# Mask products of both query halves in four row groups, with parts of the v product between them

## The chip, the cores and the metric

The kernel runs on one core of one Trainium2 chip. The metric is the device time of one execution in microseconds. A core has a matrix engine (PE, which reads its operands from SBUF and writes to PSUM), a vector engine (DVE), a scalar engine (ACT), a third elementwise engine (POOL) and SyncE (SP). Each takes its instructions in the order in which the program puts them there; semaphores tie them together. DMAs are issued from the queues of SP, ACT and POOL.

## The reference

Two blocks in a row: an attention in which a query sees only the keys with the same 6-bit hash, then a two-layer feed-forward block with a learned slope.

```python
q_bits = (np.einsum('bhsd,dk->bhsk', q, proj) > 0)     # 4 batches, 8 heads, 768 tokens, width 64, 6 bits
k_bits = (np.einsum('bhsd,dk->bhsk', k, proj) > 0)
mask = q_bucket[:, :, :, None] == k_bucket[:, :, None, :]
scores = np.where(mask, scale * np.matmul(q, k.transpose(0, 1, 3, 2)), -1000000000.0)
attn = np.exp(scores - max); attn = attn / (sum(attn) + 1e-09)
x = np.matmul(attn, v)                                  # to (3072, 512)
h = x @ w_in
out = (np.maximum(h, 0.0) + alpha * np.minimum(h, 0.0)) @ w_out
```

All inputs and outputs are float32.

## The kernel before

`fast_path` does the work; `general_path` runs only if the inputs are out of the range that `fast_path` takes. Heads are taken in 16 **pairs** (`pi`), the two heads `s` of a pair on partitions 0 to 63 and 64 to 127. The loop over pairs is the attention stage, which takes the first 305 us or so; then the feed-forward stage begins, with the two layers in blocks.

Everything wrapped in `do(...)` keeps its program order on its engine. What isn't, most DMAs for instance, is put among it by the framework.

**One pair on PE.** The 768 keys are six key tiles `kc` of 128 (`NC`), the 768 queries are two halves `g` of 384 (`NCH`, `CW`). A *cell* is one `(kc, g)`; `CELLS` lists the twelve, `(0,0), (0,1), (1,0)` and so on.

- `scores` (L778), for each cell: first the **bit product**, one bf16 matmul for each head, then the full-precision product `kT` by `qT`, one float32 matmul for each head, added to the same PSUM tile (L786; each head's operands stand on 64 rows of the array). The bit product adds a penalty where the hashes differ, so that the exponential there is nothing. The bits of keys (`kb`) and queries (`qb`) take 12 of the 64 rows of each head; the rest is zero. ACT then takes the exponential of both heads at once into `pts[kc]` (L789).
- `hash_bits` (L727): the hash products of the next pair's keys and queries (L734), their signs on ACT (`hr`, L740), and six DMAs from POOL and two from ACT that bring them to `qb` and `kb` (L747). `qb` has two buffers, `kb` one.
- `attend` (L811): the product with v, the **v cells**. Twelve cells of four float32 matmuls, each on 32 columns of the array (L819), accumulate in `av`, which has one buffer in PSUM.
- `totals` (L825): eight products with ones (L832) of the summed exponentials into `sm`.

PSUM: a score tile takes two banks (`two_banks`, three buffers, which `hs` and `sm` share), `av` takes two.

**One pair on DVE and POOL.** `divide(pi - 1)` (L836) turns the totals of the previous pair into reciprocals: DVE's transpose `st` (L846), `rc`, `rr` and `vs` (L851); then on POOL `weight_sums`, which forms one difference of the first layer's weights (L664) if one is due, and four small copies that spread `rr` over partitions (L855, L856); then on DVE whatever is passed as `between`, the transpose `dn` (L858) and the quotient `x` (L864), which is the last reader of `av`. `x` goes to DRAM from SP. `between` is `weight_begin`: the transpose of the next pair's keys `kT` (L713, `turn_blocks`), two steps of rounding a piece of the weights (`weight_clamp` L611, `weight_parts` L617), in four pairs a difference of x's (`sum_x`), and the first addition of exponentials (`add_first`, `accp`, L797). Then follow on DVE the end of that weight piece (`weight_sum`, L642 and L645), the other additions (`add_third` L805, `add_last` L801 and L802, `add_total` L808), the second piece of the pair, and the transpose of the queries of the pair after the next. `load_weight` fetches further pieces from POOL's queue.

In program order a pair is: twelve score cells, `divide` of the previous pair with `weight_begin` inside it, weight work and additions, `hash_bits`, twelve v cells, `totals`.

Of the kernel before, what the change touches and what calls it, by code (L numbers as in the profile page):

```python
# [8 lines left out]
F32 = mybir.dt.float32  # L9
# [3 lines left out]
AF = mybir.ActivationFunctionType  # L13
# [394 lines left out]
def fast_path(  # L408
# [12 lines left out]
    nc = tc.nc  # L421
    P = 128
    B, H, S, D = q.shape
    NB = proj.shape[1]
# [4 lines left out]
    NC = S // P  # L429
# [3 lines left out]
    NCH = NC // CH  # L433
# [162 lines left out]
    def weight_abs(i, engine=None):  # L596
        i = order[i]
        lo, hi = halves(i)
        wx[i] = pool.tile([P, 512], F32, name=f"wx{i}", tag="wx")
        wr[i] = pool.tile([P, 512], I32, name=f"wr{i}", tag="wr")  # L600
        do(ACT.activation(wr[i], lo, AF.Copy, scale=2.0 ** -29))  # L601
        if engine is DVE:
            do(DVE.tensor_scalar(wx[i].bitcast(U32), hi, 0x7FFFFFFF, None, op0=ALU.bitwise_and))
            return
        do(ACT.activation(wx[i], hi.bitcast(F32), AF.Abs))
# [86 lines left out]
    def two_banks(name):  # L692
        return psum.tile([P, 2, 512], F32, name=name, tag="sc", bufs=3)
# [33 lines left out]
    def hash_bits(pi):  # L727

        both = two_banks(f"hs{pi}")
        ps = both[:, 0, :CW]  # L730
        for half in range(2):
            for n, name in enumerate("kq"):
                c = D * n + 32 * half
                do(PE.matmul(  # L734
                    ps[c : c + 32], wh2, tr[name, pi][:, half * CW : (half + 1) * CW], start=True, stop=True,
                ))
        if pi == 2:
            do(PE.transpose(both[:, 1, :NF], alpha16, ident[:NF, :NF]))
        raw = pool.tile([P, CW], BF16, name=f"hr{pi}", tag="hr", bufs=1)
        do(ACT.activation(raw, ps, AF.Sign, bias=hb2))  # L740
        if pi == 2:
            do(DVE.tensor_copy(alpha, both[:, 1, :NF]))
        bits["q", pi], bits["k", pi] = qbs[pi % 2], kb
        for name, half, queue in (("k", 0, nc.scalar), ("q", 0, nc.gpsimd), ("q", 1, nc.gpsimd), ("k", 1, nc.gpsimd)):
            for s in range(2):
                c = D * "kq".index(name) + 32 * half + NB * s
                queue.dma_start(  # L747
                    bits[name, pi][D * s : D * s + 2 * NB, half * CW : (half + 1) * CW], raw[c : c + 2 * NB],
                )

    def hash_first(half):

# [25 lines left out]
    def scores(pi, cells):  # L778
        for kc, g in cells:
            sc = two_banks(f"sc{pi}_{kc}_{g}")  # L780
            ks = slice(kc * P, (kc + 1) * P)
            qs = slice(g * CW, (g + 1) * CW)
            for what, first in ((bits, True), (tr, False)):
                for s in range(2):
                    r = slice(D * s, D * s + D)
                    do(PE.matmul(  # L786
                        sc[:, s, :CW], what["k", pi][r, ks], what["q", pi][r, qs], start=first, stop=not first,
                    ))
            do(ACT.activation(pts[kc][:, g, :, :CW], sc[:, :, :CW], AF.Exp, scale=SCALE / DOWN))  # L789


    def p(kc):
        return pts[kc].rearrange("p g s w -> p (g s) w")[:, :, :CW]

    def add_first(pi):
        accp[pi] = pool.tile([P, 2 * NCH, CW], F32, name=f"accp{pi}", tag="accp", bufs=1)
        do(DVE.tensor_tensor(accp[pi], p(0), p(1), op=ALU.add))  # L797
# [10 lines left out]
        do(DVE.tensor_tensor(accd[pi], accd[pi], accp[pi], op=ALU.add))  # L808


    def attend(pi):  # L811

        av[pi] = psum_av.tile([P, 2, 512], F32, name=f"av{pi}", tag="av")
        for kc in range(NC):
            for g in range(NCH):
                w = CW + 1 if g == 0 else CW
                for s in range(2):
                    for t in range(0, D, 32):
                        do(PE.matmul(  # L819
                            av[pi][D * s + t : D * s + t + 32, g, :w], nat["v", pi][:, s, kc * D + t : kc * D + t + 32],  # L820
                            pts[kc][:, g, s, :w], start=(kc == 0), stop=(kc == NC - 1),
                        ))
# [13 lines left out]
    def divide(pi, between=lambda: None):  # L836

        b, hp = pairs[pi]  # L840
        n = CW // 32
        a = pool.tile([P, CW], F32, name=f"st{pi}", tag="st", bufs=1)
        r = pool.tile([P, n], F32, name=f"rc{pi}", tag="rc")
        rr = pool.tile([P, NCH, n], F32, name=f"rr{pi}", tag="rr")
        d = pool.tile([P, NCH, CW], F32, name=f"dn{pi}", tag="dn", bufs=1)
        do(DVE.transpose(a, sums[pi][:, 0, :CW]))  # L846
        do(DVE.tensor_scalar(r, a.rearrange("p (n w) -> p n w", w=32)[:, :, 0], S * EPS, None, op0=ALU.add))
        for g in range(NCH):
            do(DVE.reciprocal(rr[:, g], r))
        vsum[pi] = pool.tile([P, 1], F32, name=f"vs{pi}", tag="vs")  # L850
        do(DVE.tensor_scalar(vsum[pi], av[pi][:, 0, CW : CW + 1], EPS, None, op0=ALU.mult))  # L851
        weight_sums(1, vsum[pi])
        for q0 in (0, D):
            q1 = q0 + 32
            do(POOL.tensor_copy(rr[q0 : q0 + 32, 1], rr[q1 : q1 + 32, 1]))  # L855
            do(POOL.tensor_copy(rr[q1 : q1 + 32, 0], rr[q0 : q0 + 32, 0]))  # L856
        between()
        do(DVE.transpose(  # L858
            d.rearrange("p g w -> p (g w)"),
            rr.rearrange("p g n -> p (g n)").unsqueeze(2).to_broadcast([P, NCH * n, 32]),  # L860
        ))

        x = mid.tile([P, NCH, CW], F32, name=f"x{pi}", tag="x", bufs=1)
        do(DVE.scalar_tensor_tensor(x, av[pi][:, :, :CW], vsum[pi], d, op0=ALU.add, op1=ALU.mult))  # L864
        nc.sync.dma_start(x_s[b, hp], x.rearrange("p g w -> p (g w)"))
# [641 lines left out]
    for pi in range(NPAIR):  # L1507
        i = 2 * pi
        if pi == 12:
            now_stored.append(pi)  # L1510

        def weight_end(i):
            weight_sums(1, weight_sum(i))
            weight_group(i)
            load_weight(i + 3)

        def weight_begin():
            if pi == 1:
                weight_end(1)
                turn_blocks(2, "q")  # L1520
            if pi + 1 < NPAIR:
                turn_blocks(pi + 1, "k")
            weight_clamp(i)
            weight_parts(i)
            if pi in (6, 9, 12, 15):
                sum_x(0, (6, 9, 12, 15).index(pi), DVE)
            add_first(pi)

        if pi:
            scores(pi, CELLS)  # L1530
            divide(pi - 1, weight_begin)
            if pi == 1:
                weight_abs(3)
        else:
            rest = [c for c in CELLS if c not in ahead]
            scores(pi, rest[:4])
            weight_abs(0, DVE)
            scores(pi, rest[4:])
            add_first(pi)
            weight_clamp(0)  # L1540
            weight_parts(0)
        weight_sum(i)
        weight_group(i)
        load_weight(i + 3)
        if pi > 1:
            weight_clamp(i + 1)
        add_third(pi)
        add_last(pi)
        add_total(pi)
        if pi == 0:  # L1550
            weight_abs(1, DVE)
            weight_clamp(1)
        if pi == 1:
            weight_clamp(i + 1)
        weight_parts(i + 1)
        if pi:
            weight_end(i + 1)
        if pi + 1 < NPAIR:
            hash_bits(pi + 1)
            do(ACT.activation(tr["q", pi + 1], tr["q", pi + 1], AF.Copy, scale=DOWN))  # L1560
        if 0 < pi < NPAIR - 2:
            turn_blocks(pi + 2, "q")
        attend(pi)
        if pi + 1 == NPAIR:
            now = ff1(0, 0)
            now.step(1)
        totals(pi)
        if pi + 1 == NPAIR:
            now.step(5)
            divide(pi)  # L1570
        else:
            weight_abs(i + 2)
        if pi + 2 < NPAIR:
            load(pi + 2, "v")
        while stores_due and pi < 10:
            stores_due.pop(0)()
        if pi in (9, 12, 15):
            load_w((9, 12, 15).index(pi))
        if pi in (3, 4, 6, 9):
            load_x(0, {3: 0, 4: 3, 6: 2, 9: 1}[pi])  # L1580
        for name in "qk":
            magnitude(pi, name)
            if pi + 3 < NPAIR:
                load(pi + 3, name)
        if stores_due and pi == 11:
            stores_due.pop()()
        if 0 < pi < NPAIR - 1:
            weight_abs(i + 3)
# [142 lines left out]
```

## Time and profile before

| | |
|---|---|
| median of 3 runs | 858.42 us (857.66 to 858.5) |
| the profiled execution | 859.28 us, its span 857.5 us |
| PE busy | 847.5 us, 99% of the span |
| DVE busy | 772.4 us, 90% |
| ACT busy | 405.5 us, 47% |
| POOL busy | 163.9 us, 19% |
| granted PE clock | 0.998 |
| score products in float32 (L786) | 768 matmuls, mean 482 ns |
| bit products (L786) | 384 matmuls, mean 324 ns |
| v products (L819) | 1536 matmuls, mean 485 ns |

The span is the time from the first to the last instruction of the profiled execution, which stands beside the time that the same execution took on the device. Matmuls are pipelined: one starts before the one before it has ended, and those on different rows or columns of the array overlap. So a duration in the table is not what a matmul adds; the distance from start to start is. The page's chain of waits is empty for this execution, so it is read from the engines' timelines.

### The profile page before, as it was taken

To read this page: it belongs to the slowest core of one execution; us is meant where nothing else is said; L and a number is where in the kernel's file an instruction comes from. 1 tells how busy PE (TensorE), PEld (TensorE's weight loads), DVE (VectorE), ACT (ScalarE), POOL (GpSimd) and SP (SyncE) were. 2 spreads that over 40 slices of the span, in tenths; PEclk is the share of its full clock that TensorE was granted. 3 is DMA by queue.
4 is the path that set the end of the run, shared out by engine and by line. 5 is a ranking of instruction groups with operands and counts; after the bars stand their busy time and mean duration, and the time that the engine had idled before them with its cause. 6 is when DMAs were issued, how large, how long until landed. Compare 5 with 4: busy or idle time off the path is not lost.

```text
span 857.5 us, 15370 instructions
## 1 busy us (share of the span) xinstructions
PE 847.5 (99%) x5674; PEld 600.0 (70%) x5674; DVE 772.4 (90%) x1251; ACT 405.5 (47%) x754; POOL 163.9 (19%) x321
## 2 busy tenths in 40 slices
PE   9999999999999999999999999999999999999996
PEld 4444444444445445559998769999778999687996
DVE  6999999999999987889998989998879998879996
ACT  7787788876867842331115441114452114352111
POOL 1322434424424401210006200002100000300001
PEclk9999999999999999999999999999999999999999
DMA  8965779879698437784444844335833435830242
GB/s 198 179 151 132 188 180 240 166 200 252 147 220 198 153 123 271 235 273 166 166 126 120 296 141 135 113 115 179 287 130 114 145 117 171 262 118 22 99 164 63
DMA packets 181765, 144.85 MB, mean 169 GB/s; under 512 B 121536, under 2 KB 161648, under 8 KB 178096
## 3 DMA queue, kind: packets, MB, share of 16 engines
q1 hardware_dynamic: 166496, 113.15, 46.7%
q0 software_dynamic: 12176, 29.29, 11.2%
q10 hardware_dynamic: 3008, 1.33, 0.6%
q8 instruction: 47, 0.77, 0.4%
q14 instruction: 38, 0.31, 0.1%
HBM read 111.16 MB, written 31.46 MB: 166 GB/s over the span
## 4 chain that ended last, share of the span: by engine, by line


## 5 line engine op out<-in xcount | busy, mean ns | idle before, releaser
L786 PE MATMUL sc<-qT,kT 64*128 64x384 f32 x768 | 155.1, 482 | 0.0
L789 ACT ACTIVATE pt<-sc 128x768 f32<-128x768 f32 x192 | 151.6, 810 | 3.4 <-PE sc L786 3.3
L819 PE MATMUL av<-pt,vn 128*32 128x385 f32 (+1 forms) x1536 | 127.1, 485 | 0.0
L819 PEld LDWEIGHTS av<-pt,vn 128*32 128x32 f32 x1536 | 50.2, 109 | 73.4 <-issue 70.0
L786 PEld LDWEIGHTS sc<-qT,kT 64*128 64x128 f32 x768 | 68.4, 187 | 35.8 <-issue 35.0
L1411 POOL DMA_DIRECT2D out_dram<-o x52 | 28.3, 553 | 337.9 <-DVE o L1404 336.4
L786 PE MATMUL sc<-qb,kb 64*128 64x384 bf16 x384 | 63.3, 324 | 0.6 <-DVE st L846 0.4
L976 DVE TENSOR_TENSOR g<-g,g 128x768 f32<-128x768 f32 (+1 forms) x80 | 62.8, 793 | 0.7
L1357 DVE TENSOR_TENSOR gs<-g,gs 128x768 f32<-128x768 f32 x56 | 53.3, 952 | 1.0
L1357 DVE TENSOR_TENSOR gs<-g 128x768 f32<-128x768 f32 x56 | 53.3, 951 | 0.0
L786 PEld LDWEIGHTS <-kb 64*128 64x128 bf16 x384 | 20.7, 94 | 36.2 <-issue 13.2
L1349 DVE TENSOR_TENSOR ws<-wl 128x512 f32<-128x512 f32 x56 | 38.4, 686 | 6.8 <-DMA wl<-w_out_s 6.8
L601 ACT ACTIVATE wr<-raw 128x512 int32<-128x512 uint32 x32 | 22.1, 691 | 32.7 <-DVE wso L645 17.0
L747 POOL DMA_DIRECT2D qb<-hr x60 | 30.1, 508 | 23.0 <-ACT hr L740 23.0
L797 DVE TENSOR_TENSOR accp<-pt,pt 128x1536 f32<-128x1536 f32 x16 | 28.1, 1758 | 4.3 <-ACT pt L789 4.3
L802 DVE TENSOR_TENSOR accd<-accd,pt 128x1536 f32<-128x1536 f32 x16 | 28.1, 1759 | 1.7
L808 DVE TENSOR_TENSOR accd<-accd,accp 128x1536 f32<-128x1536 f32 x16 | 28.1, 1758 | 0.6
L995 DVE SCALAR_TENSOR_TENSOR g<-h,alpha 128x384 f32<-128x384 f32 x39 | 23.9, 613 | 5.2 <-ACT h L988 4.9
L805 DVE TENSOR_TENSOR accp<-accp,pt 128x1536 f32<-128x1536 f32 x16 | 28.0, 1753 | 0.0
L801 DVE TENSOR_TENSOR accd<-pt,pt 128x1536 f32<-128x1536 f32 x16 | 28.0, 1751 | 0.0
L1560 ACT ACTIVATE qT<-qT 128x768 f32<-128x768 f32 x15 | 12.7, 844 | 26.4 <-DMA kb<-hr 17.4
L642 DVE SCALAR_TENSOR_TENSOR wx<-raw,wx 128x512 uint32<-128x512 uint32 x32 | 22.7, 709 | 0.5
(494 smaller groups left out, 1914.2 us busy)
## 6 DMA issues: line engine op xcount, KB each, us to landing
wi<-w_in_s SPq DMA_DIRECT2D x32, 512.0 KB
wl<-w_out_s SPq DMA_DIRECT2D x16, 1024.0 KB
wl<-w_out_r SPq DMA_DIRECT2D x12, 1024.0 KB
raw<-in_moe_w_in_dram POOLq DMA_DIRECT2D x15, 512.0 KB, 5.1
raw<-in_moe_w_out_dram POOLq DMA_DIRECT2D x14, 512.0 KB, 5.3
w_in_s<-wsi SPq DMA_DIRECT2D x16, 448.0 KB
qn<-in_q_dram SPq DMA_DIRECT2D x64, 96.0 KB
vn<-in_v_dram SPq DMA_DIRECT2D x16, 384.0 KB
```

The lines of the kernel that those rows point to most:

```text
L747: queue.dma_start(bits[name, pi][D * s : D * s + 2 * NB, half * CW : (half + 1) * CW], raw[c : c + 2 * NB],)
L786: do(PE.matmul(sc[:, s, :CW], what["k", pi][r, ks], what["q", pi][r, qs], start=first, stop=not first,))
L789: do(ACT.activation(pts[kc][:, g, :, :CW], sc[:, :, :CW], AF.Exp, scale=SCALE / DOWN))
L797: do(DVE.tensor_tensor(accp[pi], p(0), p(1), op=ALU.add))
L801: do(DVE.tensor_tensor(accd[pi], p(3), p(4), op=ALU.add))
L802: do(DVE.tensor_tensor(accd[pi], accd[pi], p(5), op=ALU.add))
L808: do(DVE.tensor_tensor(accd[pi], accd[pi], accp[pi], op=ALU.add))
L819: do(PE.matmul(av[pi][D * s + t : D * s + t + 32, g, :w], nat["v", pi][:, s, kc * D + t : kc * D + t + 32], pts[kc][:, g, s, :w], start=(k ...
L976: do(DVE.tensor_tensor(new_g(b, to)[:, at], g_m[b, x][:, at], g_m[b, y][:, at], op=ALU.subtract))
L1349: do(DVE.tensor_tensor(t, w2[b, n, x], w2[b, n, y], op=op))
L1357: do(DVE.tensor_tensor(t, g2[b, n, x], g2[b, n, y], op=ALU.subtract))
L1411: pinned(b + 1 < B and queue is nc.sync, queue.dma_start(out_v[b, ch * CH + c].rearrange("(w r) d -> r w d", r=32)[:, :, cols], src[32 * a ...
```

## The change

From the third pair on (`pi > 1`), the bit products of the last three key tiles are made for both query halves together. `hash_bits` puts a second copy of the key bits (columns of the last three key tiles) and of the query bits (second half) on rows 32 to 43 of each head's 64. The new `scores_both` multiplies 32 rows at a time: for each half and head one group of 32 rows, four matmuls into two PSUM tiles. Then come the float32 products and the exponential of each half as before. Before each of these three steps stands one v cell of the same pair, so `attend` runs in parts, and `CELLS[3:]` are left for its old place. `divide` of the previous pair now stands after the first six score cells in the program, with only `turn_blocks` as its `between`; the rest of `weight_begin` follows it. Pairs 0 and 1 keep their order; rows 32 to 63 of the key bits' first half are set to zero once.

```diff
@@ hash_bits
+        for name in "kq":
+            for s in range(2):
+                c = D * "kq".index(name) + 32 + NB * s
+                to = D * s + 32
+                nc.gpsimd.dma_start(bits[name, pi][to : to + 2 * NB, CW:], raw[c : c + 2 * NB])
@@
+    def scores_both(pi, kc):
+
+        sc = [two_banks(f"sc{pi}_{kc}_{g}") for g in range(NCH)]
+        ks = slice(kc * P, (kc + 1) * P)
+        for g in range(NCH):
+            for s in range(2):
+                r = slice(D * s + 32 * g, D * s + 32 * g + 32)
+                do(PE.matmul(
+                    sc[g][:, s, :CW], bits["k", pi][r, ks], bits["q", pi][r, g * CW : (g + 1) * CW],
+                    start=True, stop=False,
+                ))
+        for g in range(NCH):
+            for s in range(2):
+                r = slice(D * s, D * s + D)
+                do(PE.matmul(
+                    sc[g][:, s, :CW], tr["k", pi][r, ks], tr["q", pi][r, g * CW : (g + 1) * CW],
+                    start=False, stop=True,
+                ))
+            do(ACT.activation(pts[kc][:, g, :, :CW], sc[g][:, :, :CW], AF.Exp, scale=SCALE / DOWN))
@@
-    def attend(pi):
+    def attend(pi, parts):
 
-        av[pi] = psum_av.tile([P, 2, 512], F32, name=f"av{pi}", tag="av")
-        for kc in range(NC):
-            for g in range(NCH):
+        if pi not in av:
+            av[pi] = psum_av.tile([P, 2, 512], F32, name=f"av{pi}", tag="av")
+        for kc, g in parts:
+            if True:
@@ weight_begin
             if pi == 1:
                 weight_end(1)
                 turn_blocks(2, "q")
-            if pi + 1 < NPAIR:
                 turn_blocks(pi + 1, "k")
@@ the loop over pairs
-        if pi:
+        if pi > 1:
+            scores(pi, CELLS[:6])
+            divide(pi - 1, lambda: turn_blocks(pi + 1, "k") if pi + 1 < NPAIR else None)
+            weight_begin()
+            for kc in range(3, NC):
+                attend(pi, CELLS[kc - 3 : kc - 2])
+                scores_both(pi, kc)
+        elif pi:
             scores(pi, CELLS)
             divide(pi - 1, weight_begin)
-            if pi == 1:
-                weight_abs(3)
+            weight_abs(3)
         else:
...
+            for s in range(2):
+                do(POOL.memset(kb[D * s + 32 : D * s + 64, :CW], 0.0))
...
-        attend(pi)
+        attend(pi, CELLS[3:] if pi > 1 else CELLS)
```

## The prediction

> **What bounds the kernel now.** I read the page's busy shares and slices first, then the timelines of PE, DVE and POOL through one pair of heads, then the DMA answers for the mask bits. The page says which engine is full:
>
> ```profile
> PE 847.5 (99%) x5674; PEld 600.0 (70%) x5674; DVE 772.4 (90%) x1251; ACT 405.5 (47%) x754; POOL 163.9 (19%) x321
> PE   9999999999999999999999999999999999999996
> PEclk9999999999999999999999999999999999999999
> ```
>
> PE has no gap and the full clock, so whatever PE issues more, or waits for, in the attention stage is added to the time. Matmul rows overlap, so I count from start to start. This is the PE timeline of one pair's end and the next one's start (columns: start us, us, engine, line, operation, names, shapes, count):
>
> ```profile
> 76.39 0.32 PE L786 MATMUL sc<-qb,kb 64*128 64x384 bf16 x2
> 76.55 0.81 PE L786 MATMUL sc<-qT,kT 64*128 64x384 f32 x4
> 77.29 0.51 PE L734 MATMUL hs<-kT,wh 128*32 128x384 f32 x1
> ...
> 77.64 0.49 PE L734 MATMUL hs<-kT,wh 128*32 128x384 f32 x1
> ...
> 77.96 7.94 PE L819 MATMUL av<-pt,vn 128*32 128x385 f32 x96
> 85.71 0.83 PE L832 MATMUL sm<-accd,ones 128*32 128x384 f32 x8
> 86.48 0.34 PE L786 MATMUL sc<-qb,kb 64*128 64x384 bf16 x2
> 86.65 0.81 PE L786 MATMUL sc<-qT,kT 64*128 64x384 f32 x4
> 87.29 0.33 PE L786 MATMUL sc<-qb,kb 64*128 64x384 bf16 x2
> ```
>
> Within one shape nothing is lost: bits to full precision 0.165 (86.48 to 86.65), full precision to the next bits 0.642, so 0.807 a cell; a v cell is 7.75/12 = 0.646. Where the shape changes, something is: 76.55 to 77.29 is 0.74 for 0.642 of work, and 85.71 to 86.48 is 0.77 for the 0.645 that eight such products take. A change of shape costs 0.10 to 0.125. A pair has two of them: 12 x 0.807 + 0.10 + 0.67 + 7.75 + 0.77 = 18.97, and the sm rows of successive pairs do lie 18.98 apart.
>
> DVE runs through the same pair with hardly more room (its timeline):
>
> ```profile
> 87.03 0.54 DVE L846 STREAM_TRANSPOSE st<-sm 128x384 f32<-128x384 f32 x1
> 88.09 0.10 DVE L851 TENSOR_SCALAR vs<-av 128x1 f32<-128x1 f32 x1
> 88.11 0.97 DVE L713 STREAM_TRANSPOSE kT<-kn 128x768 f32<-128x768 f32 x1
> 89.00 0.65 DVE L611 TENSOR_SCALAR_CACHE_REDUCE wx<-wx 128x512 f32<-128x512 f32 x1
> ...
> 92.45 0.97 DVE L858 STREAM_TRANSPOSE dn<-rr 128x768 f32<-128x768 f32 x1
> 93.45 1.02 DVE L864 SCALAR_TENSOR_TENSOR x<-av,vs,dn 128x768 f32<-128x768 f32 x1
> ```
>
> Between vs and dn stands POOL, which spreads the reciprocals and, in 8 of the 14 pairs that change, first forms a weight sum (its timeline):
>
> ```profile
> 88.46 1.28 POOL L664 TENSOR_TENSOR wsi<-wsi 128x512 f32<-128x512 f32 x1
> 89.81 0.36 POOL L855 COPY rr<-rr 32x12 f32<-32x12 f32 x1
> 90.20 0.19 POOL L856 COPY rr<-rr 32x12 f32<-32x12 f32 x1
> 90.44 0.19 POOL L855 COPY rr<-rr 32x12 f32<-32x12 f32 x1
> 90.67 0.19 POOL L856 COPY rr<-rr 32x12 f32<-32x12 f32 x1
> ```
>
> POOL ends at 90.86, 2.67 after vs. DVE doesn't notice: kT, the clamp, the shift and the 1.76 accp addition lie between. PE doesn't notice either: x ends at 94.47, and the next v product, which overwrites av, starts at 96.94.
>
> **The change part by part**, for a pair from 2 to 15. T is the start of its first score (86.48 here).
>
> *Bits.* Three times, two steps of 0.165 become one: -3 x 0.165 = -0.495. That four row groups run side by side is shown by no row; two row groups do here, and four column groups do (four hs products start within 0.02). From below the gain is 0, from above 0.495; the rows nearest to it say full, which I take.
>
> *Changes of shape.* v cells (128*32) now stand between scores (64*128), with 32-row bits between. In order: scores, v, bits, scores, v, bits, scores, v, bits, scores, hash: 11 changes with the one at the start, against 2. Of the nine added, six are between shapes that the rows show, at 0.10 to 0.125. Three go from 32-row bits to 64-row scores, which nothing shows: from below 0, since both span 128 columns; from above the largest change in the trace, f_0a to sm, 1.49 from start to start for 1.29 of work, 0.20. I take 0.12, as every change of shape in the trace lies near it. Sum 9 x 0.12 = 1.08. With the bits +0.585 a pair, x 14 = +8.2.
>
> A rule of the Trainium skill speaks against the change here: "TensorEngine Tiling (Array Packing)", Key Properties, says that going to another tiling mode, not just another tile, drains the engine. The rows above agree with it for the shapes that they hold; by the rule all nine changes count, and without it the three that no row shows could be left out, which would make the sum 42 x 0.12 = 5.0 less. "TensorE: Matmul & The Clock Gate", Measured speedup vs the span model, has four row tiles at 3.07 times, not 4; a step would then be an estimated 0.165 x 4/3.07 = 0.215, and the sum 42 x 0.05 = 2.1 more.
>
> *divide() ahead of the weight work, v before the last keys.* The first v cell overwrites av, so PE must now wait for x before the seventh score cell. PE comes there at T + 6 x 0.807 + 0.11 = T + 4.95. x: the totals end 0.06 after T (85.71 + 0.83), st starts 0.05 later (hs to its reader takes as much), vs ends 1.16 on, POOL 2.67, dn at once (0.03), x ends 2.02 after: T + 5.99, and some 0.06 to PE. PE stands 1.1 in the eight pairs with a sum. In the six without, POOL needs 0.93 (126.24 to 127.12), x is there at T + 4.3, and nothing waits. Queued behind the waiting product are all bits and scores of three key tiles and the hash; ACT's exponentials of these and DVE's accd wait for them in turn.
>
> The other side of it: DVE lost its cover and stands from kT's end (89.00) to 90.89, 1.9 a pair. Its own work is 18.3 (18.98 less 0.66 of waiting), so its round is 20.2 with a sum. PE's is 18.98 + 0.585 + 1.1 = 20.7: DVE keeps up, comes to st on time, and it is PE that waits. Its last work of a pair ends some 0.4 before the next totals are there. The addition of accd with the last key tile starts at T + 14.2, just when its last exponential ends.
>
> *POOL and the bits.* Four more DMAs a pair, 0.51 each, behind the six on POOL. They end 2.0 later, 0.4 before the next T; the weight load (0.55) and the sum of the pair's end (0.18, 1.28) come behind them, so that in six pairs vs finds POOL busy some 0.2 longer. Waits for x: 2 x 1.1 + 6 x 1.3 = +10.0.
>
> The last DMA starts 1.8 + 9 x 0.5 = 6.3 after the hash. In the quietest pairs one lands 1.6 after its issue; in the others the first takes 2 to 6.4 and the rest follow at 0.17 to 0.2. So the tenth lands 7.9 to 9.9 after the hash. The second score cell, which reads its rows, comes 0.67 + 9 x 0.646 + 0.77 + 0.81 = 8.06 after. Laid over the first landings of the 14 pairs this makes 5 in all, of which all but 1.1 falls where PE would wait for x anyway: +1.1. From below 0; from above 0.8 in each pair, 11.
>
> *At nothing:* the two memsets of kb (at most 0.74 each, the row of qb's, covered by POOL's wait for hr; 1.5 once without); turn_blocks of k, which stays at its place; the store of x on SP, which only moves forward; the v tile, loaded a pair ahead; psum, as scores_both needs two of three buffers and ACT, at 0.78 a cell, catches up during the v cells.
>
> **Sum:** 8.2 + 10.0 + 1.1 = 19.3. The profiled execution took 859.28, with a span of 857.5; the span becomes 876.8. The median of the runs is 858.42, 0.9 less than that execution: 877.7, said as 878.
>
> **Rivals.**
> - *Only the changes of shape.* x comes in time, as in the pairs without a sum, for instance if POOL's copies run before its sum. For: six pairs behave so. Against: the order on POOL stands in divide(). 858.4 + 8.2 + 1 = 868.
> - *The bits land late.* If each DMA takes the middle 4.0 from its own issue, the last lands 1.8 + 4.5 + 4.0 = 10.3 after the hash, 2.25 late in every pair, and the wait for x hides in it: 858.4 + 8.2 + 31.5 = 898. Against: the DMAs of one group now land 0.2 apart though issued 0.5 apart.
> - *Four row groups don't run together.* The change then doesn't do what it says: 877.7 + 6.9 = 885.
> - *Faster: the changes of shape are free at the new places.* If a change costs nothing when the next weights go to other rows, PE gains 14 x 0.495 = 6.9, hence 851.5. It decides below 0.495/9 = 0.055 a change, and only if x is early too: with x as late as above it ends at 861.5. Against: every change in the trace, whatever its rows and columns, costs 0.09 or more.
>
> **How the numbers follow.** Forecast 0.62, only shapes 0.16, late bits 0.12, four groups not together 0.04, free changes 0.06. The likeliest gives 878. Its low end: six changes at 0.105, three at 0, 8 waits of 0.9: 858.4 + 1.9 + 7.2 = 867.5. Its high end: nine at 0.14, waits of 1.5, landings 11: 858.4 + 10.7 + 12 + 11 = 892. I widen to 866 for the second case; what is left out is most of the late bits and the faster case, some 0.17. A difference under 0.2%, 1.7, can't be told from none. Of the free changes' 0.06, 0.01 is within that: faster 0.05, same 0.02, slower 0.93.
>
> **What would show it.** Right: the stretch from v cell to 32-row bits to scores has some 0.12 over its work at each step; PE's first v cell waits some 1.1 on DVE's x in eight pairs; dn waits on POOL some 1.9 there; sm rows lie 19.5 apart without a sum and 20.7 with one. Wrong: no gap at the changes, or bits of 0.33 for four, or a wait of the second score cell on a DMA in most pairs, or st waiting on nothing while sm waits on accd, which would make DVE the bound.

## The result, and the profile after

The changed kernel takes 971.8 us (median of 6 runs, 966.2 to 974.1) against 858.6: 1.131 times as long, interval 1.128 to 1.134. The forecast was 878, with a range up to 892. It is slower, as forecast, but by far more: 113 us lost where 19 were forecast.

The page of the changed kernel, its lines for PE, the granted clock, and the costliest wait of PE (line, engine, operation, names, shapes, count | busy us, mean ns | idle before, and what ended it):

```profile
PE 895.9 (92%) x5674; PEld 615.6 (63%) x5674; DVE 777.1 (80%) x1251; ACT 403.3 (41%) x754; POOL 184.7 (19%) x383
...
PE   9978778788887788999999999999999999999997
...
PEclk9978888998887889999999999999999999999999
...
L791 PE MATMUL sc<-qb,kb 64*128 64x384 bf16 x216 | 54.1, 394 | 68.0 <-DMA qb<-hr 67.9
```

PE, which had no gap before, now has gaps in the attention stage, and its clock is no longer full there. 68 us of the gaps end with a DMA from `hr` to `qb`: a copy of the query bits. The timeline of PE shows where it stands, from the end of one pair on:

```profile
241.98 0.83 PE L858 MATMUL sm<-accd,ones 128*32 128x384 f32 x8
242.74 0.34 PE L791 MATMUL sc<-qb,kb 64*128 64x384 bf16 x2
242.91 0.81 PE L791 MATMUL sc<-qT,kT 64*128 64x384 f32 x4
243.56 0.32 PE L791 MATMUL sc<-qb,kb 64*128 64x384 bf16 x1
247.65 0.47 PE L791 MATMUL sc<-qb,kb 64*128 64x384 bf16 x1 [3.77 <-DMA qb<-hr]
247.65 1.75 PE L791 MATMUL sc<-qT,kT 64*128 64x384 f32 x4
249.09 0.63 PE L791 MATMUL sc<-qb,kb 64*128 64x384 bf16 x2
249.41 1.59 PE L791 MATMUL sc<-qT,kT 64*128 64x384 f32 x4
250.69 0.63 PE L791 MATMUL sc<-qb,kb 64*128 64x384 bf16 x2
```

It is the second score cell, the first that reads the second half of the queries. Its first head goes ahead at 243.56; the other head stands for 3.8 until its copy has landed. And the cells after it come at 249.09 and 250.69, 1.60 apart, where 0.807 is the rule: PE runs at half its clock. Why the copy is late stands in POOL's timeline of the same pair (the DMA rows are their issue):

```profile
237.29 1.98 POOL L747 DMA_DIRECT2D qb<-hr  x4 [6.56 <-ACT hr L740]
239.26 1.24 POOL L747 DMA_DIRECT2D kb<-hr  x2
240.49 0.98 POOL L754 DMA_DIRECT2D kb<-hr  x2
241.47 0.51 POOL L754 DMA_DIRECT2D qb<-hr  x1
241.96 0.54 POOL L587 DMA_DIRECT2D raw<-in_moe_w_out_dram  x1
242.50 0.50 POOL L754 DMA_DIRECT2D qb<-hr  x1
```

The ten copies don't stand together. The weight load of 512 KB (L587) has been put in ahead of the last one; in pairs with a sum due POOL's sum goes in there as well. From issue to landing the trace has for the ninth copy (241.47), and then for the tenth (242.50), 9 KB like it but behind the load:

```profile
DMA to landing us min/median/max: 1.6/1.6/1.6
```

```profile
DMA to landing us min/median/max: 5.1/5.1/5.1
```

Thirteen of the 14 changed pairs have a load ahead of the last copy (in pair 2, of the last three), and their second cell waits 3.3 to 6.4. In the last pair no load is due: there the tenth copy lands 3.1 after its issue and the cell waits 1.2.

The granted clock in three stretches around that wait (stretch: length, busy of PE, PEld, DVE, ACT, POOL with instructions, PEclk, DMA share, GB/s):

```profile
238.00:245.70 7.70, 5.88 (x67) 2.19 (x60) 7.33 (x13) 5.65 (x10) 5.75 (x14) 1.00 0.40 102
245.70:252.50 6.80, 4.85 (x19) 3.09 (x20) 3.17 (x6) 1.62 (x2) 0.00 (x0) 0.50 1.14 334
252.50:259.00 6.50, 6.50 (x53) 2.78 (x50) 5.33 (x6) 4.19 (x6) 0.54 (x1) 1.00 0.91 166
```

Some 1.8 us into the wait (from 243.9) the clock is halved, and it stays so for 6.8, of which PE works nearly 5.

By the last totals the changed kernel is 115.7 behind (430.2 against 314.5). PE's gaps make 67 of it. The order of the products makes 11: where nothing waits a pair takes 19.84 in the second run below, against 18.98, 13 times (pair 2 took 19.90 before). Of the other 37 most is the clock: through the stage it is halved for 96 us, and PE works in some 63 of these, half of which, 32, is what it loses. Some 6 are not put down to anything.

### The profile page after: what moved, and what is told of

Its sections match the earlier page's. It is cut to its first block, busy times and chain, and to the rows that moved or that the text cites. A ratio compares the mean times of both kernels' runs of the same rounds, so it can differ in the third digit from the quotient of the medians.

```text
span 972.3 us, 15503 instructions
## 1 busy us (share of the span) xinstructions
PE 895.9 (92%) x5674; PEld 615.6 (63%) x5674; DVE 777.1 (80%) x1251; ACT 403.3 (41%) x754; POOL 184.7 (19%) x383
## 4 chain that ended last, share of the span: by engine, by line
## 5 line engine op out<-in xcount | busy, mean ns | idle before, releaser
L845 PE MATMUL av<-pt,vn 128*32 128x385 f32 (+1 forms) x1536 | 135.8, 488 | 0.0
L791 PE MATMUL sc<-qT,kT 64*128 64x384 f32 x432 | 120.1, 616 | 0.0
L791 PE MATMUL sc<-qb,kb 64*128 64x384 bf16 x216 | 54.1, 394 | 68.0 <-DMA qb<-hr 67.9
L845 PEld LDWEIGHTS av<-pt,vn 128*32 128x32 f32 x1536 | 45.8, 109 | 80.2 <-issue 79.8
L791 PEld LDWEIGHTS sc<-qT,kT 64*128 64x128 f32 x432 | 56.1, 244 | 50.0 <-issue 50.0
L810 PE MATMUL sc<-qT,kT 64*128 64x384 f32 x336 | 65.6, 509 | 0.0
L810 PEld LDWEIGHTS sc<-qT,kT 64*128 64x128 f32 x336 | 29.0, 186 | 18.0 <-issue 7.3
L884 DVE STREAM_TRANSPOSE dn<-rr 128x768 f32<-128x768 f32 x16 | 15.6, 978 | 18.5 <-POOL rr L882 18.0
```

The costliest lines, as they stand in the source:

```text
L791: do(PE.matmul(sc[:, s, :CW], what["k", pi][r, ks], what["q", pi][r, qs], start=first, stop=not first,))
L810: do(PE.matmul(sc[g][:, s, :CW], tr["k", pi][r, ks], tr["q", pi][r, g * CW : (g + 1) * CW], start=False, stop=True,))
L845: do(PE.matmul(av[pi][D * s + t : D * s + t + 32, g, :w], nat["v", pi][:, s, kc * D + t : kc * D + t + 32], pts[kc][:, g, s, :w], start=(k ...
```

## The experiments

Theory Q: the tenth copy lands late because the weight load stands ahead of it on POOL's queue, PE stands at the second cell, and the clock halves. Rival S: the changes of shape and the wait for x. Rival C: four more copies a pair are late wherever they stand.

**Which copy is last (e1).**

```diff
-        for name in "kq":
+        for name in "qk":
             for s in range(2):
                 c = D * "kq".index(name) + 32 + NB * s
```

> The changed kernel with the second copies of the query bits issued ahead of those of the key bits, so that the one copy that falls behind the weight load on POOL's queue is a key copy, which is not read before the seventh score cell. Theory Q (the query copy lands late because a 512 KB weight load and a POOL sum stand in front of it, PE stands at the second score cell, and the clock halves after that): the waits of the second cell go, the granted clock is 1.00 through the attention stage, and the time falls to 875 to 890. Rival S (the added changes of shape and the wait for x make the loss): it stays at 960 to 980. Rival C (four more copies a pair are late wherever they stand): it stays above 930.

Measured: 896.6, 1.044 times the time before (1.043 to 1.046). Two thirds of the loss go with the order of four small DMAs. It is over the 890 that Q named: four cells still wait for query copies (8.5 us), late key copies hold up a few bit products of 32 rows (1.5 us of PE, 2.7 of its weight loads), and the wait for x, up to 1.2, shows again. After the two longest of these waits (4.6 and 3.0) the clock is halved, for 10 us together. Q stands against S and C; C would have been above 930.

**Another queue for the copies (e2).**

```diff
-                nc.gpsimd.dma_start(bits[name, pi][to : to + 2 * NB, CW:], raw[c : c + 2 * NB])
+                nc.sync.dma_start(bits[name, pi][to : to + 2 * NB, CW:], raw[c : c + 2 * NB])
```

> The changed kernel with the four second copies issued from SP's queue in place of POOL's. Theory Q: no wait of the second score cell on a copy, clock 1.00, 873 to 885, a little under the run with the order swapped, as POOL is free for its sum and copies. Rival S: 960 to 980. Rival C: above 930, as the copies still share the DMA engines.

Measured: 885.5, 1.030 (1.027 to 1.032). Apart from three pairs with 1.8 to 4.1 of waiting and a halved clock after it, pairs take 19.84 without a sum of weights and 20.79 with one. In those three POOL issued its weight load ahead of at least the last of SP's copies; in the other eleven it issued it after all four, or none. So this run also has the two smaller terms pure: 0.86 a pair for the order of the products, 0.95 for the wait for x.

**v cells between, no row groups (e3).**

```diff
-        for name in "kq":
-            for s in range(2):
-                c = D * "kq".index(name) + 32 + NB * s
...
-                scores_both(pi, kc)
+                scores(pi, [(kc, 0), (kc, 1)])
```

> The changed kernel without the row groups: no second copies, the bits of the last three key tiles in 64 rows as before, one v cell ahead of each of these tiles, divide early. It adds six changes of shape a pair at 0.14 to 0.15 and the wait for x in the eight pairs where POOL has a sum due. Theory Q: 872 to 884, clock 1.00. Rival S: above 940.

Measured: 876.0, 1.020 (1.018 to 1.022), all by clock 1.00. Pairs take 19.71, and 20.66 with a sum. The wait for x is plain in its timeline of PE:

```profile
91.94 0.81 PE L786 MATMUL sc<-qT,kT 64*128 64x384 f32 x4
93.62 0.85 PE L840 MATMUL av<-pt,vn 128*32 128x385 f32 x8 [0.87 <-DVE x L885]
94.41 0.34 PE L786 MATMUL sc<-qb,kb 64*128 64x384 bf16 x2
```

The v cell would have come at 92.68, 0.74 after the score; it starts at 93.62.

**The copies alone (e4).** The kernel before, with the copies and the memsets and nothing else.

```diff
+        for name in "kq":
+            for s in range(2):
+                c = D * "kq".index(name) + 32 + NB * s
+                to = D * s + 32
+                nc.gpsimd.dma_start(bits[name, pi][to : to + 2 * NB, CW:], raw[c : c + 2 * NB])
...
+            for s in range(2):
+                do(POOL.memset(kb[D * s + 32 : D * s + 64, :CW], 0.0))
```

> The kernel before with nothing but the four second copies of the bits (and the memsets); the order of the pairs and the products stay. Theory Q: the last copy stands behind the weight load and POOL's sum here too, so the second score cell waits 4 to 7 in most pairs and the clock halves after it: 940 to 985. Rival S: 857 to 862. Rival C: 900 to 985, so this run tells Q and C from S, and the first two runs tell Q from C.

Measured: 952.4, 1.110 (1.108 to 1.113). Four DMAs of 9 KB a pair, which no product needs here, cost 94 us: 83% of the change's loss. (The products read the rows that the copies fill, so they wait.) In the last pair, where no load is due, the tenth copy lands 1.6 after its issue, nothing waits, and the pair takes 19.94 as before. The page of this run:

```profile
PEclk9988889898898898999999999999999999999999
...
L791 PE MATMUL sc<-qb,kb 64*128 64x384 bf16 x384 | 84.3, 358 | 61.9 <-DMA qb<-hr 61.9
```

**The weight load off the queue (e5).**

```diff
-    def load_weight(i, queue=nc.gpsimd):
+    def load_weight(i, queue=nc.sync):
```

> The changed kernel with the weight loads inside the loop issued from SP's queue, the ten bit copies staying on POOL's queue in the changed kernel's order. Theory Q (what holds the last copy is the 512 KB load ahead of it on the same queue): the last copy lands 1.6 to 3 after its issue, the second cell waits under 1 in most pairs, clock near 1.00, 873 to 890. Rival C2 (POOL's own queue of ten copies is too slow, load or not): above 930.

Measured: 910.5, 1.060 (1.057 to 1.062): over Q's 873 to 890, under C2's 930. In nine pairs the last copy lands 1.6 to 3.0 after its issue and the cell waits at most 1.2; in none of them did SP issue a weight load in the 6 us ahead of that copy. In the other five the cell still waits 2 to 6. In four of these SP had issued a load 0.8 to 4.8 ahead of the last copy, and the copy took 4.1 to 5.7, though the load now stood on another queue (in the fifth the load was 5.4 ahead, and the copy took 3.7). One of the four, in the timelines of SP, POOL and PE:

```profile
245.56 0.33 SPq L587 DMA_DIRECT2D raw<-in_moe_w_in_dram  x1
245.87 1.03 POOL L754 DMA_DIRECT2D qb<-hr  x2
250.14 0.70 PE L791 MATMUL sc<-qb,kb 64*128 64x384 bf16 x2 [2.06 <-DMA qb<-hr]
```

So a load issued ahead of the copy holds it up, and Q's words "on the same queue" are not borne out: what helped the nine pairs is that the load came after their copies. The load of the DMA engines plays a part too: they are busy for 0.86 to 0.99 of the stretch in three of the five pairs, where even the first copies take 5, and for about half in the other two, against 0.25 to 0.35 in pairs with short waits. That is read from the trace, and no run shows it by itself.

**Row groups alone (e6).** Bits of both halves in 32 rows, copies from SP, `divide` and all v cells at their old places.

```diff
-            divide(pi - 1, lambda: turn_blocks(pi + 1, "k") if pi + 1 < NPAIR else None)
-            weight_begin()
             for kc in range(3, NC):
-                attend(pi, CELLS[kc - 3 : kc - 2])
                 scores_both(pi, kc)
+            divide(pi - 1, lambda: (turn_blocks(pi + 1, "k") if pi + 1 < NPAIR else None, weight_begin()))
...
-        attend(pi, CELLS[3:] if pi > 1 else CELLS)
+        attend(pi, CELLS)
```

> Row groups alone: the last three key tiles by 32-row bits for both halves, no v cell between, divide and all v cells at their old places, second copies from SP. Shape theory from the runs so far: a tile loses about 0.10 from scores to 32-row bits and 0.21 from there to scores and gains 0.165, so +0.43 a pair, 864 to 866, and no wait for x. Rival (PSUM): with no v cell to cover them, two score tiles at once out of three buffers make PE wait for ACT, 0.3 a tile or more: 868 to 880, with waits of PE on ACT's exponentials in the trace.

Measured: 876.7, 1.021 (1.020 to 1.023), every changed pair 20.26 but the last (21.22, 19.94 before). The rival was right. Its PE timeline:

```profile
95.09 1.56 PE L810 MATMUL sc<-qT,kT 64*128 64x384 f32 x8
96.58 0.67 PE L803 MATMUL sc<-qb,kb 32*128 32x384 bf16 x4
97.18 1.56 PE L810 MATMUL sc<-qT,kT 64*128 64x384 f32 x8
```

The four bit products take 0.60 here against 0.27 with a v cell ahead: the second of the two score tiles is not free yet. ACT's timeline has its two exponentials on the tiles before from 96.05 to 97.56, the first until 96.86; two of the four bit products start at 96.58, the other two at 96.91. The v cells between are worth these 0.33 a key tile.

**POOL's sum after its copies (e7).** On e3:

```diff
-        weight_sums(1, vsum[pi])
         for q0 in (0, D):
...
             do(POOL.tensor_copy(rr[q1 : q1 + 32, 0], rr[q0 : q0 + 32, 0]))
+        weight_sums(1, vsum[pi])
```

> The third run (v between, bits in 64 rows) with POOL's weight sum put after the four small copies in divide. If the 0.95 by which the pairs with a sum are longer there is the wait for x behind POOL's sum, all pairs take 19.71: 858.6 + 14 x 0.73 = 869, 867 to 871, and PE's v cell waits on nothing. Rival (the wait is DVE's own lateness or the shapes): it stays at 874 to 877.

Measured: 869.0, 1.012 (1.010 to 1.014). Nearly all pairs take 19.71. The 0.95 was POOL's sum in the chain from `vs` to x, 7 us in all.

**Cells of the first half first (e8).**

```diff
-            scores(pi, CELLS[:6])
+            scores(pi, [(kc, g) for g in range(NCH) for kc in range(CH)])
```

> The changed kernel with the first six score cells in the order of the halves, so that three cells, not one, stand ahead of the one that reads the late copy; queue and copies as in the changed kernel. Theory Q: each wait is 1.6 shorter, about 3 to 4 a pair less than 5, and the clock loss shrinks more than in proportion, as waits below some 3.4 leave the clock alone: 905 to 945. Rival (the halved clock has another cause than the wait, such as 32-row products): the granted clock stays at 0.95 over the run, and only the 22 of shorter waits are gained, 947 to 953.

Measured: 943.1, 1.100 (1.096 to 1.105). PE's waits on the copies fell from 68 to 45, as expected from 1.6 a pair; the time the clock is halved fell from 96 to 61, not more than in proportion. Half the expectation failed: waits of 2.0 to 2.4 still halve the clock.

**Both waits taken away (e9).** The changed kernel with the edits of e1, e2 and e7 together.

> The changed kernel with both kinds of wait taken away: the second copies from SP with those of the queries first, and POOL's weight sum after the four small copies. What is left is the row groups, the nine changes of shape and the v cells between: 19.84 a pair against 18.98, so 858.4 + 14 x 0.86 = 870.5; with one or two pairs whose copies are still late behind other traffic 870 to 880. No wait of a v cell on x. If the row groups or the order gained anything that the waits had hidden, it would be below 866.

Measured: 872.5, 1.015 (1.014 to 1.017). Of the 14 changed pairs eleven take 19.84, one 20.15, the last 20.80 (19.94 before), and one 23.75, as SP issued its copies behind other loads. What is left is a loss by the shapes: the idea itself costs some 11 us (0.86 in 13 pairs).

**The wait filled (e10).** Twenty repeats of a bit product ahead of the second cell, whose result is overwritten.

```diff
+            for _ in range(20 if pi > 1 and (kc, g) == (0, 1) else 0):
+                for s in range(2):
+                    r = slice(D * s, D * s + D)
+                    do(PE.matmul(sc[:, s, :CW], bits["k", pi][r, ks], bits["q", pi][r, :CW], start=True, stop=True))
```

> The changed kernel with twenty repeats of a bit product (3.3 of PE work, its result overwritten) ahead of the second score cell of each changed pair, where PE otherwise stands waiting for the late copy. If the halved clock is caused by that standing and costs some 35 of the 113 by itself, the clock stays at 1.00 or nearly so and the time falls to 932 to 950 though PE does more; the waits that are left are about 1 to 3 a pair. Rival (the clock halves for another reason, or the slow cells hide in the wait): the time rises or stays, 965 to 1015.

Measured: 957.6, 1.116 (1.113 to 1.119). More work for PE, 14 us less time than the changed kernel. The expected range was missed: I took the waits for 3 to 6 and thought that 3.3 of filling would leave too little to halve the clock; in seven of 14 pairs it left 2 to 3, and the clock was still halved, for 27 us in place of 96. The DMAs are the same in this run, so their traffic isn't what halves the clock. That the clock follows PE's standing is shown; its price, some 32 to 36, is worked out and was not measured free of the waits.

No version of this idea beats the kernel before, so none was run as such.

## Why the prediction was wrong

*What bounds the kernel* was right: PE, with nothing to spare. So was the reading that each wait and each change of shape adds to the time.

*The step that failed* is the one on POOL and the bits. It put the four copies "behind the six on POOL", and then "the weight load (0.55) and the sum of the pair's end (0.18, 1.28) come behind them". It took the order in which the copies and the load stand in the timeline before for the order after. There the load came 3.8 after the last of six copies:

```profile
98.06 2.00 POOL L747 DMA_DIRECT2D qb<-hr  x4 [1.83 <-ACT hr L740]
100.06 1.00 POOL L747 DMA_DIRECT2D kb<-hr  x2
104.85 0.55 POOL L587 DMA_DIRECT2D raw<-in_moe_w_in_dram  x1 [3.79 <-DVE wx L642]
```

They are not wrapped in `do(...)`, so their place is not the program's, and the tenth copy went behind a 512 KB load. It was priced at +1.1, from above 11; the waits measured 67, and 62 with the copies alone. The prediction had named the sign of it, "a wait of the second score cell on a DMA in most pairs". The rival of late bits had the right place, the second cell, but took 4.0 from issue to landing, and 0.12 of the chance; it gave 898. Neither had a term for the clock, 32 to 36 more. With such a wait in every pair the forecast's bounds could not hold.

*Changes of shape*: right in kind, low in size: +11 for a forecast of +8.2. Nine changes and the bits came to 0.86 a pair where 0.585 was forecast. By its parts, in the PE timeline of e9 (a float32 product stands there as two matmuls, one after the other):

```profile
92.84 0.81 PE L791 MATMUL sc<-qT,kT 64*128 64x384 f32 x4
93.58 0.85 PE L845 MATMUL av<-pt,vn 128*32 128x385 f32 x8
94.36 0.34 PE L803 MATMUL sc<-qb,kb 32*128 32x384 bf16 x4
94.63 1.56 PE L810 MATMUL sc<-qT,kT 64*128 64x384 f32 x8
96.12 0.85 PE L845 MATMUL av<-pt,vn 128*32 128x384 f32 x8
```

Scores to v is 0.74 for 0.645: 0.10. v to bits is 0.78 to 0.79 for 0.646: 0.14; the prediction counted this among the changes that its rows show, but none of them holds 32-row bits. Bits to scores is 0.27: 0.105, if the step itself takes the 0.165 of two row groups. And the eight score products take 1.49 to the next v cell, for 1.29 and the 0.10 of that change, another 0.10: the first of their four steps takes 0.43, not 0.32. The second weight load starts 0.11 after the first there, where the later ones start along with the matmul before; that this is the reason is not shown. So from 32-row bits to float32 scores the price is 0.21, just over the bound of 0.20; I took 0.12. Three times 0.10 + 0.14 + 0.21 less 0.165 is the 0.86. The rule of the Trainium skill, "TensorEngine Tiling (Array Packing)", Key Properties, held at all nine places, those without a row among them.

*The bits* were right: four row groups do run together (their starts lie within 0.01, and each takes 0.33 as in the two groups before). But a step saved is 0.165 and a change of shape into scores costs 0.21: row groups lose 0.13 a pair even with the v cells between (19.84 against 19.71).

*The wait for x* was right in mechanism and near in size: 0.95 in eight pairs, 7 us, for 1.1 to 1.3 and 10. In the changed kernel itself it doesn't show: the second cell has waited longer already. DVE's wait on POOL, 1.64 in e3, is the 1.9 that was forecast for an early st.

*The faster rival*, free changes, is out: each change cost 0.10 to 0.21.

## What to carry to other kernels

A small DMA that another engine waits for must be placed by what is issued ahead of it, on its own queue or on another, and where a framework orders it, the order has to be read after the change, not taken from the trace before: here copies of 9 KB, the last of them issued behind 512 KB, cost 94 us by themselves. A wait of PE cost more than its length here once it filled half of a clock stretch. And here a step saved by row groups, 0.165, did not pay the two changes of shape around it, 0.14 and 0.21; whether a longer run of products in the new shape pays was not tried.

## What the runs showed of the hardware

The granted clock changed only at steps of a grid of 3.41 us, counted from the trace's clock marks. Taking the full-speed stretches of that grid in the attention stages of the changed kernel and its variants, every one with 1.79 us or more of PE standing was followed by half the clock (over 50 of them, in seven kernels), and none with 1.69 or less was (30 with over 0.7); two lie between, 1.73 and 1.76, one of each kind. So about half a stretch of standing is enough. In e8, for instance (stretches as above):

```profile
77.60:81.00 3.40, 1.77 (x14) 1.04 (x12) 2.95 (x5) 1.47 (x3) 0.00 (x0) 1.00 1.10 225
81.00:84.40 3.40, 3.40 (x29) 1.35 (x24) 2.15 (x2) 2.30 (x4) 0.00 (x0) 1.00 0.97 177
```

```profile
231.20:234.60 3.40, 1.30 (x12) 0.85 (x10) 3.33 (x6) 1.00 (x3) 0.00 (x0) 1.00 1.07 337
234.60:238.00 3.40, 3.40 (x19) 1.26 (x15) 1.59 (x2) 2.12 (x3) 0.00 (x0) 0.51 1.13 336
```

PE stands 1.63 in the first pair's stretch and keeps its clock; it stands 2.10 in the other's and loses half of it for the next. The Trainium skill, "TensorE: Matmul & The Clock Gate", Why this matters for your kernels, warns of gaps over some 3 us; in e2 one wait of 1.79 was enough, and the measurement decides.
